# A transformer block on one core: the normed h of the MLP turned by VectorE's 32x32 blocks, with the sum stored in another order and a strided moving side

## The chip, the core and the metric

The kernel runs on one core of a Trainium2 chip. The core has five engines that work at the same time and are tied together by semaphores: TensorE (matmuls and transposes, results into PSUM), VectorE, ScalarE, GpSimd, and SyncE, which here only issues transfers between the chip's memory (DRAM) and the core's own memory (SBUF). In the profile they are PE (with PEld, its loading of weights), DVE, ACT, POOL and SP. The metric is the device time of one execution in microseconds (us); lower is better.

## The reference

An attention block and an MLP, each behind a layernorm, on 2048 tokens of width 1024, all in float32:

```python
h  = x + attention(layernorm(x), wqkv, w_phi, wo)     # 32 heads of 32, feature map by two softmaxes
h2 = h + relu(layernorm(h) @ w1) @ w2                 # w1: 1024 x 3584, w2: 3584 x 1024
```

The change lies between the sum h and the product with w1: h is summed, its mean and variance per token are taken, it is normed, and turned so that the width lies on the 128 partitions (TensorE sums over partitions).

## The kernel before, in words

Each float32 product is made of three products of split operands in the fp32r format: a high part, and the low part that is left (`mm3`, lines 180 to 183: high by high, high by low, low by high). The split costs a copy on ScalarE and a subtraction on VectorE or GpSimd. A 128x512 result lies in one PSUM bank. The banks are named `mm` (4), `tp` (2) and `ac` (2).

The stages, in order of time: projections to k, v and q for all tokens; attention, overlapped with the output projection (`wo_item`, 128 tokens by 512 columns each, eight `mm3`); the MLP's up projection (`up_item`), in two halves b = 0, 1 of 1024 tokens; then its down projection.

Up and down projection use a scheme with seven instead of eight products of quarter matrices (Strassen's, Winograd's form). One half has 1024 tokens and a width of 1024, so it is a matrix of four quarters of 512x512. Seven operands are formed from them: the quarters themselves and sums and differences of them. For the turned h they are called m = 1, 5, 6, 2, 7, 3, 4 (`UP`).

The path of h, tile by tile (a tile has 128 tokens, number t):

- `wo_load` loads x in halves of 512 columns, `wo_add` adds the product to it on VectorE (line 728), `wo_store` stores the half to the DRAM tile `hd[t]`.
- `ln_pair(b, i, stage)` takes two tiles, of the token quarters r = 0 and 1, at the same place i. Eight pairs in all: four with b = 0 beside the output projection, four with b = 1 during the up projection. Stage 0 loads both tiles (line 214), 1 takes the statistics on VectorE (`bn_stats`, line 220), 2 makes scale and bias on GpSimd (lines 229 to 231), 3 norms on ScalarE (line 243). Stages 4 to 7 turn both tiles on TensorE: four groups of four 128x128 transposes (lines 250 and 758) into a `tp` bank, and a copy back by ScalarE (lines 252 and 759). Stage 7 also makes two of the sums on VectorE (lines 760 and 761), stage 8 two more on GpSimd (lines 766 and 767).
- `ln_store` stores the seven operands of the pair to DRAM tiles `hs[b, m]`, `h_load` brings them back by operand and half g into the low part of `hT[m]`, `h_high` and `h_low` split them.
- `up_item` multiplies: the weights w are the stationary side, `hT[m][:, s, k, :]`, 512 contiguous columns (tokens), is the moving side.
- At the end `d_load` loads h from `hd` once more, and `d_add` adds the down projection to it.

The order of the instructions on each engine is written out by hand. TensorE's list of work is made of items. A step is one `mm3` within an item; `when(step, f, ...)` puts a piece of work behind that step. All the other engines get their instructions in the order of these steps, each engine executes its own in that order, and waits stand in that order too. `wo0` and `up0` are the first steps of output and up projection. `LN2` holds the steps of the stages of a pair, counted from `wo0 + 64 + 40 i` for b = 0 and `up0 + 60 + 68 i` for b = 1; its last number is that of the stores.

SP issues nearly all the transfers, in order as well: the raw weights (six buffers, loaded as they come free), x, h, the seven operands, the results.

Of the kernel before, what the change touches and what calls it, by code (L numbers as in the profile page):

```python
# [15 lines left out]
P = 128  # L16
# [123 lines left out]
def kernel(  # L140
# [56 lines left out]
    hd = [dram.tile([P, D], F32, name=f"hd{t}") for t in range(NT)]  # L197
# [17 lines left out]

    def ln_stats(key):
        src = xin[key]
        st = lnp.tile([P, 2, 6], F32, name="st", bufs=4)
# [21 lines left out]
    def ln_norm(key):  # L240
        sc, src = xst.pop(("s", key[1]) if key[0] == "x" and key[1] >= HT else key), xin.pop(key)
        xnt[key] = src if key[0] == "h" else fp_ln.tile([P, D], F32, name="xn")
        act.activation(xnt[key], src, AF.Identity, bias=sc[:, 1:2], scale=sc[:, 0:1])

    def ln_turn(key, j, dst=None):
# [5 lines left out]
        if dst is None:  # L251
            act.activation(xn[:, j * 512:(j + 1) * 512], pt.rearrange("p k n -> p (k n)"), AF.Copy)
            return
# [446 lines left out]
    def wo_load(t, hf):  # L700
        xh[t, hf] = hp.tile([P, 512], F32, name="xh", bufs=5)
        sp.dma_start(xh[t, hf], x[t * P:(t + 1) * P, hf * 512:(hf + 1) * 512])

# [22 lines left out]

    def wo_add(t, hf):
        v.tensor_add(xh[t, hf], wo_ps.pop((t, hf)), xh[t, hf])

    def wo_store(t, hf):  # L730
        sp.dma_start(hd[t][:, hf * 512:(hf + 1) * 512], xh.pop((t, hf)))

    def ln_pair(b, i, stage):

        keys = [("h", HT * b + 4 * r + i) for r in range(2)]
        if stage == 0:
            for key in keys:  # L740
                ln_load(key, [hd[key[1]]])
        elif stage == 1:
            for key in keys:
                ln_stats(key)
        elif stage == 2:
            for key in keys:
                ln_power(key)
        elif stage == 3:
            for key in keys:
                ln_norm(key)  # L750
        elif stage in (4, 5, 6):
            ln_turn(keys[stage // 6], stage != 4)
        elif stage == 7:
            x1, x2 = (xnt[key] for key in keys)
            s12 = (mp or hp).tile([P, 2, 512], F32, name="s12", bufs=1)
            pt = tp_bank()
            for k in range(4):
                pe.transpose(pt[:, k * P:(k + 1) * P], x2[:, k * P:(k + 1) * P], ident)  # L758
            act.activation(x2[:, 0:512], pt, AF.Copy)
            v.tensor_add(s12[:, 0, :], x2[:, 0:512], x2[:, 512:])  # L760
            v.tensor_sub(x2[:, 0:512], x1[:, 0:512], x2[:, 0:512])
            sums[b, i] = s12
        elif stage == 8:
            x1, s12 = xnt[keys[0]], sums[b, i]
            s4 = (mp or hp).tile([P, 512], F32, name="s4l", bufs=1)
            pool.tensor_tensor(out=s12[:, 1, :], in0=s12[:, 0, :], in1=x1[:, 0:512], op=ALU.subtract)
            pool.tensor_tensor(out=s4, in0=x1[:, 512:], in1=s12[:, 1, :], op=ALU.subtract)
            sums[b, i] = s12, s4

    def ln_store(b, i, j):  # L770

        x1, x2 = (xnt["h", HT * b + 4 * r + i] for r in range(2))
        s12, s4 = sums[b, i]
        m, t = ((1, x1[:, 0:512]), (5, s12[:, 0, :]), (6, s12[:, 1, :]), (2, x1[:, 512:]), (7, x2[:, 0:512]),
                (3, s4), (4, x2[:, 512:]))[j]
        sp.dma_start(hs[b, m][:, i, :], t)
# [3 lines left out]
    def h_load(b, m, g):  # L780

        lo = hT[m][:, 1, :, 2 * g * P:2 * (g + 1) * P].rearrange("p k (i n) -> p k i n", i=2)
        for i in range(2):
            sp.dma_start(f32(lo[:, :, i, :]), hs[b, m][:, 2 * g + i, :].rearrange("p (k n) -> p k n", k=4))

    def h_parts(m, g):

        return (hT[m][:, s, :, 2 * g * P:2 * (g + 1) * P] for s in range(2))
# [531 lines left out]
```

## Time and profile before

| | us |
|---|---|
| median of 3 runs | 1881.68 (1880.31 to 1882.74) |
| the profiled execution | 1881.49 |
| its span, from the first to the last instruction | 1879.7 |
| granted clock of TensorE | 1.00 throughout |
| moved by DMA | 433.21 MB |

The profile is of one execution. It lists the busy time of each engine, the groups of instructions by line with count and mean duration, the waits, and the chain of work that ended last, followed back from the last instruction: at each step it goes to what released it, or to the instruction before it on its engine. An engine that isn't on that chain may be idle or busy without a cost. TensorE's matmuls overlap in its pipe: the duration in a group is longer than the distance from one start to the next, and it is the distance that counts. "q1" is SP's DMA queue, "q10" that of ScalarE.

### The profile page before, as it was taken

Reading aid. Unit: us, or ns where it says so; the run is one execution under the profiler, and the core shown is the slowest. Engines: PE = TensorE matmul, PEld = TensorE weight load, DVE = VectorE, ACT = ScalarE, POOL = GpSimd, SP = SyncE. Lnnn points to the kernel's source line nnn. Section 1 sums busy time; section 2 is a strip of 40 time slices with the busy share of each in tenths; the row PEclk is TensorE's granted clock in tenths of the full one; section 3 lists DMA queues with packets and bytes.
Section 4 is the critical chain, followed back from the end, with each engine's and each line's share of the span. In section 5 each row is a group of like instructions: output and inputs, shape, how many; then the busy total and the mean of one; then the engine's idle time right before and its main releaser. Section 6 shows DMA issues by size and latency. Waiting matters only on the chain.

```text
span 1879.7 us, 31869 instructions
## 1 busy us (share of the span) xinstructions
PE 1872.6 (100%) x11630; PEld 1540.3 (82%) x11630; DVE 1063.6 (57%) x1714; ACT 741.0 (39%) x1264; POOL 976.9 (52%) x956
## 2 busy tenths in 40 slices
PE   9999999999999999999999999999999999999999
PEld 7888888888888888888888888888888888888887
DVE  7788688677789777455444664444433333343333
ACT  5322244222233122355455554444444444444442
POOL 3778733677745988223343234445444444444443
PEclk9999999999999999999999999999999999999999
DMA  6889875454475567886877997877877677777775
GB/s 214 268 280 312 269 262 180 148 155 141 140 232 190 203 216 237 264 254 209 263 233 241 312 297 248 264 246 259 275 239 216 201 230 239 237 213 220 216 215 177
DMA packets 293036, 433.21 MB, mean 230 GB/s; under 512 B 24208, under 2 KB 150160, under 8 KB 292880
## 3 DMA queue, kind: packets, MB, share of 16 engines
q1 hardware_dynamic: 263712, 390.26, 65.3%
q10 hardware_dynamic: 29168, 40.93, 6.5%
q8 instruction: 91, 1.49, 0.3%
q14 instruction: 65, 0.53, 0.1%
HBM read 293.73 MB, written 137.36 MB: 229 GB/s over the span
## 4 chain that ended last, share of the span: by engine, by line
PE 98%; DVE 1%; ACT 0%; POOL 0%; DMA 0%; issue 0%; SPq 0%; DVEq 0%; POOLq 0%
PE mm L181 25%; PE mm L182 25%; PE mm L183 25%; PE ac L181 4%; PE ac L182 4%; PE ac L183 4%; PE tp L182 2%; PE tp L181 2%; PE tp L183 2%; PE tp L250 1%; PE tp L678 1%; PE ac L491 1%; PE ac L678 1%; PE tp L297 0%; DVE st L220 0%; PE tp L758 0%
## 5 line engine op out<-in xcount | busy, mean ns | idle before, releaser
L128 POOL TENSOR_TENSOR w<-raw,w 128x512 fp32r<-128x512 f32 x353 | 474.6, 1347 | 671.5 <-ACT w L124 638.0
L124 ACT ACTIVATE w<-raw 128x512 fp32r<-128x512 f32 x686 | 409.1, 626 | 491.8 <-PE mm L183 238.9
L128 DVE TENSOR_TENSOR w<-raw,w 128x512 fp32r<-128x512 f32 x333 | 275.0, 827 | 512.9 <-ACT w L124 507.3
L181 PE MATMUL mm<-w,xT 128*128 128x512 f32 x752 | 299.4, 398 | 0.0
L183 PE MATMUL mm<-w,xT 128*128 128x512 f32 x752 | 293.1, 390 | 0.0
L182 PE MATMUL mm<-w,xT 128*128 128x512 f32 x752 | 293.0, 390 | 0.0
L181 PE MATMUL mm<-hT,w 128*128 128x512 f32 x672 | 262.6, 391 | 0.0
L183 PE MATMUL mm<-hT,w 128*128 128x512 f32 x672 | 261.6, 389 | 0.0
L182 PE MATMUL mm<-hT,w 128*128 128x512 f32 x672 | 261.5, 389 | 0.0
L378 POOL TENSOR_TENSOR b<-b 128x256 f32<-128x256 f32 x168 | 129.0, 769 | 85.2 <-DMA b<-in_w_dram 75.4
L181 PEld LDWEIGHTS mm<-w,xT 128*128 128x128 f32 x752 | 141.2, 188 | 31.4 <-issue 2.2
L183 PEld LDWEIGHTS mm<-w,xT 128*128 128x128 f32 x752 | 141.2, 188 | 30.0
L182 PEld LDWEIGHTS mm<-w,xT 128*128 128x128 f32 x752 | 141.3, 188 | 28.5 <-issue 1.0
L181 PE MATMUL mm<-w 128*128 128x512 f32 x392 | 152.5, 389 | 0.0
L182 PE MATMUL mm<-w 128*128 128x512 f32 x392 | 152.5, 389 | 0.0
L183 PE MATMUL mm<-w 128*128 128x512 f32 x392 | 152.5, 389 | 0.0
L183 PEld LDWEIGHTS mm<-hT,w 128*128 128x128 f32 x672 | 126.1, 188 | 26.5
L181 PEld LDWEIGHTS mm<-hT,w 128*128 128x128 f32 x672 | 126.2, 188 | 25.8
L182 PEld LDWEIGHTS mm<-hT,w 128*128 128x128 f32 x672 | 126.2, 188 | 25.7
L480 POOL TENSOR_TENSOR zacc<-zacc,kphi 128x512 f32<-128x512 f32 x60 | 83.8, 1397 | 14.3 <-DVE kphi L472 14.3
L181 PEld LDWEIGHTS mm<-w 128*128 128x128 f32 x392 | 73.6, 188 | 15.3
L182 PEld LDWEIGHTS mm<-w 128*128 128x128 f32 x392 | 73.6, 188 | 15.3
(173 smaller groups left out, 3183.1 us busy)
## 6 DMA issues: line engine op xcount, KB each, us to landing
raw<-t SPq DMA_DIRECT2D x224, 256.0 KB, 4.0
raw<-ad SPq DMA_DIRECT2D x196, 256.0 KB, 3.0
raw<-in_w_dram SPq DMA_DIRECT2D x168, 256.0 KB, 3.2
ad<-c SPq DMA_DIRECT2D x112, 256.0 KB, 4.2
b<-in_w_dram SPq DMA_DIRECT2D x42, 512.0 KB, 5.7
t<-b SPq DMA_DIRECT2D x42, 512.0 KB, 3.6
ad<-s SPq DMA_DIRECT2D x84, 256.0 KB, 4.6
ed<-qe ACTq DMA_DIRECT2D x32, 512.0 KB, 3.9
```

What stands on the lines that cost most here:

```text
L124: nc.scalar.activation(w[:, 0, :], raw[1], AF.Copy)
L128: eng.tensor_tensor(out=w[:, 1, :], in0=raw[1], in1=w[:, 0, :].bitcast(F32), op=ALU.subtract)
L181: pe.matmul(ps, a_hi, b_hi, start=first, stop=False, skip_group_check=more)
L182: pe.matmul(ps, a_hi, b_lo, start=False, stop=False, skip_group_check=more)
L183: pe.matmul(ps, a_lo, b_hi, start=False, stop=last, skip_group_check=more)
L250: pe.transpose(pt[:, k, :], xn[:, (4 * j + k) * P:(4 * j + k + 1) * P], ident)
L378: pool.tensor_tensor(out=tsum[j, *out], in0=tsum[j, *a], in1=tsum[j, *b], op=ALU.subtract)
L480: pool.tensor_tensor(out=zacc[s], in0=zacc[s], in1=phi_of[key], op=ALU.add)
L491: pe.matmul(kv_ps[s][g][32 * i:32 * (i + 1), 0:64], vt[:, 32 * h:32 * (h + 1)], phi[:, 64 * h:64 * (h + 1)], start=first, stop=last)
L678: pe.matmul(banks[g][32 * c:32 * (c + 1), r * P:(r + 1) * P], kvL[rows, 4 * q + 2 * sd + h // 4, 32 * (h % 4):32 * (h % 4 + 1)], phT[rows, ...
```

## The change

VectorE's `transpose` turns each 32x32 block of a tile in its place. It takes a column inside a block to a row, and leaves the blocks where they are. For the width to come to lie on the partitions in the right order, h is stored so that the loads put the blocks where they are needed.

- `wo_add` writes the sum in another order of columns into a new tile `xo` (2 buffers; `xh` has 3 instead of 5): a column group (k, a, i) of 4 x 4 x 32 becomes (a, k, i). `hd[t]` has the shape 4 x 128 x 2 x 128: block row a, token, half, column.
- The statistics are taken at the sum (`wo_stats`), `wo_power` makes scale and bias on GpSimd, `wo_keep` stores these two numbers per token to the DRAM tiles `shd`.
- `ln_pair` loads each tile in four pieces of 256 columns, in which a partition holds column block a of one in 32 tokens, and the scales four times, with each token's beside its piece. The norm is four instructions of 256 columns, each with its own scale. Then VectorE turns the whole 128x1024 tile in place, twice per pair. The 16 transposes on TensorE per pair and the copies from PSUM go. The sums on VectorE and GpSimd stay, on columns in two-level order.
- `h_load` loads two tiles' operands with one transfer instead of two, into a place where each partition's run is contiguous.
- The moving side of `up_item` is now 16 runs of 32 columns, 128 columns apart. The result comes out in the usual order of tokens.
- `d_load` loads h in its new order into `raw`, and the first `d_add` puts it back.
- The steps of `LN2` and of x's loads are others.

```diff
+    hd = [dram.tile([4, P, 2, P], F32, name=f"hd{t}") for t in range(NT)]
+    shd = {(b, i): dram.tile([P, 2, 2], F32, name=f"shd{b}_{i}") for b in range(2) for i in range(4)}
...
+    def turn_norm(dst, src, scale, bias):
+        for g in range(4):
+            c = slice(256 * g, 256 * (g + 1))
+            act.activation(dst[:, c], src[:, c], AF.Identity, bias=bias(g), scale=scale(g))
...
-        xh[t, hf] = hp.tile([P, 512], F32, name="xh", bufs=5)
+        xh[t, hf] = hp.tile([P, 512], F32, name="xh", bufs=3)
...
+    def by_group(ap):
+        return ap.rearrange("p (k a i) -> p k a i", k=4, a=4)
+    def by_row(ap):
+        return ap.rearrange("p (a k i) -> p k a i", k=4, a=4)
     def wo_add(t, hf):
-        v.tensor_add(xh[t, hf], wo_ps.pop((t, hf)), xh[t, hf])
+        v.tensor_add(by_row(xo[t, hf]), by_group(wo_ps.pop((t, hf))), by_group(xh.pop((t, hf))))
+    def wo_stats(t, hf):
+        st = hst[t]
+        v.bn_stats(out=st[:, 6 * hf:6 * hf + 6], in_=xo[t, hf])
+        if hf:
+            v.bn_aggr(out=st[:, 12:14], in_=st[:, 0:12].rearrange("p (j c) -> p j c", j=2))
+    def h_rows(t, hf):
+        return hd[t].rearrange("a p r c -> p a r c")[:, :, hf, :]
     def wo_store(t, hf):
-        sp.dma_start(hd[t][:, hf * 512:(hf + 1) * 512], xh.pop((t, hf)))
+        sp.dma_start(h_rows(t, hf), xo.pop((t, hf)).rearrange("p (a c) -> p a c", a=4))
+    def wo_power(t):
...
+    def wo_keep(t):
+        sp.dma_start(shd[t // HT, t % 4][:, t % HT // 4, :], hst.pop(t)[:, 14:16])
...
         if stage == 0:
+            for t in tiles:
+                hx[t] = lnp.tile([P, D], F32, name="xin")
+                src = hd[t].rearrange("a (g j) r c -> g a j (r c)", g=4)
+                for g in range(4):
+                    sp.dma_start(hx[t][:, 256 * g:256 * (g + 1)], src[g])
         elif stage == 1:
+            hsr[b, i] = sr = lnp.tile([P, 16], F32, name="st", bufs=4)
+            src = shd[b, i].rearrange("(g j) r c -> j g (r c)", g=4)
+            for a in range(4):
+                sp.dma_start(sr[32 * a:32 * (a + 1)].rearrange("p (g c) -> p g c", g=4), src)
+        elif stage in (2, 3):
+            r, sr = stage - 2, hsr[b, i]
+            turn_norm(hx[tiles[r]], hx[tiles[r]], lambda g: sr[:, 4 * g + 2 * r:4 * g + 2 * r + 1],
+                      lambda g: sr[:, 4 * g + 2 * r + 1:4 * g + 2 * r + 2])
+        elif stage in (4, 5):
+            ht = hx[tiles[stage - 4]]
+            v.transpose(ht, ht)
...
     def h_load(b, m, g):
-        lo = hT[m][:, 1, :, 2 * g * P:2 * (g + 1) * P].rearrange("p k (i n) -> p k i n", i=2)
-        for i in range(2):
-            sp.dma_start(f32(lo[:, :, i, :]), hs[b, m][:, 2 * g + i, :].rearrange("p (k n) -> p k n", k=4))
+        sp.dma_start(f32(h_parts(m, g)[1]), hs[b, m][:, 2 * g:2 * g + 2, :])
...
+    def by_token(ps):
+        return ps.rearrange("p (t j) -> p t j", j=32)
+    def h_chunk(m, s, k):
+        return hT[m][:, s].rearrange("p i (g k j) -> p k (i g) j", g=4, k=4)[:, k]
...
-            mm3(ps, w[:, 0, cols], w[:, 1, cols], hT[m][:, 0, k, :], hT[m][:, 1, k, :],
+            mm3(by_token(ps), w[:, 0, cols], w[:, 1, cols], h_chunk(m, 0, k), h_chunk(m, 1, k),
...
-        do(max(n - 2, wo_first), -1, wo_load, t, hf)
-        when(8 * n + (11 if n < wo_first + 2 else 9), wo_add, t, hf)
+        when(8 * n - 4 if n > wo_first + 1 else wo0, wo_load, t, hf)
+        late_ = 2 if n < wo_first + 2 else 0
+        when(8 * n + 9 + late_, wo_add, t, hf)
+        when(8 * n + 10 + late_, wo_stats, t, hf)
         when(8 * n + (10 if n > order[-3][1] else 14), wo_store, t, hf)
+        if hf:
+            when(8 * n + 12, wo_power, t)
+            when(8 * n + 16, wo_keep, t)
-    LN2 = ((0, 9, 12, 17, 24, 25, 26, 27, 29, 36), (0, 18, 26, 32, 40, 42, 44, 46, 50, 60))
+    LN2 = ((0, 8, 17, 19, 22, 24, 26, 28, 35), (0, 18, 32, 36, 40, 44, 48, 50, 60))
```

More of the change, by code (lines that the diff above doesn't have):

```diff
@@ new lines, in h_rows @@
+    def h_rows(t, hf):
+        return hd[t].rearrange("a p r c -> p a r c")[:, :, hf, :]
+    def wo_store(t, hf):
+        sp.dma_start(h_rows(t, hf), xo.pop((t, hf)).rearrange("p (a c) -> p a c", a=4))
+    def wo_power(t):
+        st = hst[t]
+        pool.tensor_scalar_add(st[:, 14:15], st[:, 13:14], LN_EPS)
+        pool.tensor_tensor(out=st[:, 14:15], in0=st[:, 14:15], in1=half, op=ALU.pow)
+        pool.tensor_scalar(st[:, 15:16], st[:, 12:13], st[:, 14:15], -1.0, op0=ALU.mult, op1=ALU.mult)
@@ L736, in ln_pair @@
+    def wo_keep(t):
+        sp.dma_start(shd[t // HT, t % 4][:, t % HT // 4, :], hst.pop(t)[:, 14:16])
+    hst, hst_pair, xo = {}, {}, {}
     def ln_pair(b, i, stage):
-        keys = [("h", HT * b + 4 * r + i) for r in range(2)]
+        tiles = [HT * b + 4 * r + i for r in range(2)]
         if stage == 0:
-            for key in keys:
-                ln_load(key, [hd[key[1]]])
-        elif stage == 1:
[L743 to L752, printed above, removed]
-        elif stage == 7:
[L754 to L764, printed above, removed]
@@ new lines, in ln_pair @@
+            for t in tiles:
[3 more added lines that the diff above has]
+                    sp.dma_start(hx[t][:, 256 * g:256 * (g + 1)], src[g])
+        elif stage == 1:
+            hsr[b, i] = sr = lnp.tile([P, 16], F32, name="st", bufs=4)
[9 more added lines that the diff above has]
+            v.transpose(ht, ht)
+        elif stage == 6:
+            x1, x2 = (hx[t] for t in tiles)
+            s12 = (mp or hp).tile([P, 2, 512], F32, name="s12", bufs=1)
+            v.tensor_add(by_half(s12[:, 0, :]), h_half(x2, 0), h_half(x2, 1))
+            v.tensor_sub(h_half(x2, 0), h_half(x1, 0), h_half(x2, 0))
+            sums[b, i] = s12
+        elif stage == 7:
+            x1, s12 = hx[tiles[0]], sums[b, i]
@@ L768, in ln_pair, with h_half, by_half @@
             sums[b, i] = s12, s4
+    hx, hsr = {}, {}
+    def h_half(ap, r):
+        return ap.rearrange("p (g r c) -> p g r c", g=4, r=2)[:, :, r, :]
+    def by_half(ap):
+        return ap.rearrange("p (g c) -> p g c", g=4)
     def ln_store(b, i, j):
-        x1, x2 = (xnt["h", HT * b + 4 * r + i] for r in range(2))
+        x1, x2 = (hx[HT * b + 4 * r + i] for r in range(2))
         s12, s4 = sums[b, i]
-        m, t = ((1, x1[:, 0:512]), (5, s12[:, 0, :]), (6, s12[:, 1, :]), (2, x1[:, 512:]), (7, x2[:, 0:512]),
-                (3, s4), (4, x2[:, 512:]))[j]
@@ L786, in h_parts @@
     def h_parts(m, g):
-        return (hT[m][:, s, :, 2 * g * P:2 * (g + 1) * P] for s in range(2))
+        return [hT[m][:, s, 2 * g:2 * g + 2, :] for s in range(2)]
     def h_high(m, g):
```

49 lines of the change are left out of this document (31 added, 18 removed).

## The prediction

> **What bounds the kernel now.** I read the page first, then the chain that ended last in order of time, then the views of single lines, then busy time by stretch.
>
> ```profile
> span 1879.7 us, 31869 instructions
> PE 1872.6 (100%) x11630; PEld 1540.3 (82%) x11630; DVE 1063.6 (57%) x1714; ACT 741.0 (39%) x1264; POOL 976.9 (52%) x956
> PE 98%; DVE 1%; ACT 0%; POOL 0%; DMA 0%; issue 0%; SPq 0%; DVEq 0%; POOLq 0%
> ```
>
> TensorE is busy all the time, which alone would prove little. The third line proves more: of the chain that ended last, 98% is TensorE's own instructions, so nearly the whole time it waits for nobody. What is added to its list lengthens the kernel, what is taken off shortens it, and the other engines count only where they come too late. The profiled run took 1881.49 us, 1.8 us around its span of 1879.7; the median of the runs is 1881.68, so 0.2 us are to be added at the end.
>
> What a step of TensorE costs stands in the chain, in order of time (start us, us, piece). First a turn of a tile pair beside the output projection, then one in the up projection:
>
> ```profile
> 666.84 0.23 PE mm L183
> 667.07 0.44 PE tp L250 x4
> 667.51 0.23 PE mm L181
> 667.74 0.23 PE mm L182
> 667.97 0.23 PE mm L183
> 668.20 0.44 PE tp L250 x4
> ...
> 669.33 0.44 PE tp L250 x4
> ...
> 870.96 0.44 PE tp L250 x4
> ...
> 872.79 0.44 PE tp L250 x4
> ```
>
> A group of four transposes and three matmuls take 668.20 - 667.07 = 1.13 us. For a plain matmul take a long stretch without transposes:
>
> ```profile
> 819.96 0.23 PE ac L181
> ...
> 823.81 0.23 PE ac L183
> ```
>
> These are 17 matmuls apart: 3.85 / 17 = 0.2265 us each. So the group costs 1.13 - 0.68 = 0.45 us in the first stretch. In the second, a group and six matmuls take 1.83 us, the group 0.47 us. (The 0.44 of the row leaves out what the next matmul loses; the 389 ns that the groups by line give for a matmul is its latency in the pipe.)
>
> **The change, part by part.** *Transposes off TensorE.* The turn of the normed h goes.
>
> ```profile
> L250 PE MATMUL tp<-ident,xin 128*128 128x128 f32 x96 | 14.4, 272 | 0.0
> L758 PE MATMUL tp<-ident,xin 128*128 128x128 f32 x32 | 4.8, 272 | 0.0
> ```
>
> That is 128 transposes, 32 groups of four, 16 for the first half of the tokens and 16 for the second: 16 x 0.45 + 16 x 0.47 = 14.7 us off the chain. The last column of both rows is TensorE's idle time ahead of them, nothing: all of it is work.
>
> *The strided moving side.* In its place every matmul of the up projection reads its 512 moving columns as 16 runs of 32 words, 128 words apart. The output bank is written in order, as before.
>
> ```profile
> L181 PE MATMUL mm<-hT,w 128*128 128x512 f32 x672 | 262.6, 391 | 0.0
> L181 PE MATMUL ac<-hT,w 128*128 128x512 f32 x112 | 43.9, 392 | 0.0
> ```
>
> Three lines of each: 3 x (672 + 112) = 2352 matmuls, so 1 ns each is 2.35 us, and 14.7 / 2352 = 6.2 ns each would eat the whole gain. This is the large unknown. No fp32r matmul of this trace has strided columns, but the folding one of L297 has: its moving side is w[rows, :, c, :], eight runs of 32 words, 128 words apart, in plain f32. The first three rows are its first three rounds over the 16 small tiles (timeline: start us, us); the last, from the chain, is a contiguous f32 product of 512 columns, also two instructions:
>
> ```profile
> 77.59 0.40 PE L297 MATMUL tp<-wt,wphi 32*32 32x256 f32 x2
> 77.83 0.38 PE L297 MATMUL tp<-wt,wphi 32*32 32x256 f32 x2
> 78.04 0.59 PE L297 MATMUL tp<-wt,wphi 32*32 32x256 f32 x2
> 373.59 0.86 PE tp L518 x2
> ```
>
> Contiguous, 512 columns take 0.43 us, so 256 take 0.215. Strided, 256 take 0.24 us in one round and 0.21 in the next. From above that bounds the price at 0.025 us for eight runs, 50 ns for a matmul of 16 runs, 118 us in all; from below it is nothing, as the same columns in more pieces can hardly be read faster. I take nothing: the second round is on the contiguous rate to the row's hundredth, and the first also holds the loading of 16 new tiles. The weak points are that plain f32 moves its columns at about half the rate of the up projection, and that a hundredth over eight runs is 1.25 ns per run, 20 ns per matmul, which the row can't exclude.
>
> *What is added off the chain.* Two turns of 128x1024 on VectorE for each of eight pairs, the norm in four pieces of 256 columns on ScalarE, and four copies from PSUM fewer on ScalarE per pair:
>
> ```profile
> L664 DVE STREAM_TRANSPOSE qe<-qe 128x1024 f32<-128x1024 f32 x28 | 34.2, 1227 | 12.1 <-POOL qe L658 9.5 <-POOL qe L648 1.7 <-DMA xh<-in_x_dram 1.0
> L243 ACT ACTIVATE xin<-xin,sc 128x1024 f32<-128x1024 f32 x16 | 19.3, 1236 | 13.5 <-POOL sc L231 12.7 <-DVE oT L695 0.4
> L252 ACT ACTIVATE xin<-tp 128x512 f32<-128x512 f32 x24 | 14.4, 599 | 24.2 <-PE tp L250 22.8 <-DVE qden L643 1.3
> L453 ACT ACTIVATE vt<-mm 128x256 f32<-128x256 f32 x64 | 24.5, 382 | 125.0 <-PE mm L183 125.0
> L728 DVE TENSOR_TENSOR xh<-mm,xh 128x512 f32<-128x512 f32 x32 | 21.1, 665 | 10.0 <-PE mm L183 10.0
> ```
>
> VectorE gains 16 x 1.23 = 19.6 us; ScalarE gains 16 x (4 x 0.38 - 1.24) = 4.5 us and loses 32 x 0.6 = 19.2. The statistics only move from the reloaded tile to the sum (the same 32 of them), GpSimd's power steps move with them, and the adds with regrouped operands have the same 512 columns. All of that is hidden as long as each engine keeps up with TensorE. Busy us of two stretches of 30 us beside the attention (us, PE, PEld, DVE, ACT, POOL, clock, DMA share, GB/s):
>
> ```profile
> 680.00:710.00 30.00, 30.00 (x380) 24.44 (x379) 20.03 (x36) 7.30 (x14) 25.73 (x33) 1.00 0.71 238
> 710.00:740.00 30.00, 30.00 (x380) 24.43 (x379) 23.05 (x40) 7.20 (x14) 27.02 (x34) 1.00 0.67 223
> ```
>
> VectorE stands at 23 of 30 at most. Its new turns add 2.45 us in each 36.6 us, the distance of two pairs in these SP rows (timeline):
>
> ```profile
> 644.18 1.47 SPq L214 DMA_DIRECT2D xin<-hd  x2
> 680.78 4.88 SPq L214 DMA_DIRECT2D xin<-hd  x2
> ```
>
> So VectorE goes from 77% to some 84%; if regrouping doubled the 0.665 us of the adds of L728, of which six lie in that time, it would be at 95%, still under the whole. GpSimd, at 27 of 30, is the tightest: TensorE's 36.6 us shrink by 4 x 0.45 = 1.8, and 90% become 95%. It still fits, narrowly.
>
> *Queues.* Per pair SP issues eight loads of h in quarters and four of the scales instead of two, and two stores of scales that wait for GpSimd's power. Behind them on SP stand the loads of x for the sum, the stores of h, and the raw weights. An issue is some 0.4 us, and on the other hand the up projection's h comes in 28 loads instead of 56. A late x holds VectorE's add, and behind it the turns of the attention. What margin there is shows a turn and the product that uses it, VectorE's timeline first, then the chain:
>
> ```profile
> 709.83 2.36 DVE L664 STREAM_TRANSPOSE qe<-qe 128x1024 f32<-128x1024 f32 x2
> 713.58 0.27 PE tp L678 x8
> ```
>
> The turn ends at 712.19, 1.4 us before its product, here behind the two sums of a pair; that is the tightest place I found. With one more turn of 1.23 us ahead of it, it still holds. The quarters' loads are the other unknown:
>
> ```profile
> xin<-hd SPq DMA_DIRECT2D x16, 512.0 KB, 5.2
> raw<-wpk SPq DMA_DIRECT2D x56, 128.0 KB, 3.3
> ```
>
> Quarters of 128 KB should land like the second row, in 3.3 us and a few more for their turn in the queue. The norm stands 17 steps after the load (40 steps are 36.6 us, so 15.6 us); in the up projection it stands 32 steps of three matmuls after it, 21.8 us. From below the price is nothing, from above what the second rival works out. I take nothing.
>
> *The end.* The last adds only read one operand in regrouped order. The sum is 1881.49 - 14.7 = 1866.8, and with the 0.2 us to the median **1867.0 us**, 0.8% faster.
>
> **The rivals.** *Each run of the moving side costs TensorE a start* (the one that ends slower). A contiguous column takes 226.5 / 512 = 0.44 ns. If each of 16 runs loses one column time, a matmul loses 7.1 ns, all 2352 lose 16.7 us, and the time is 1867.0 + 16.7 = 1883.7, no change. If it loses two, 33.3 us, and the time is 1900. It decides from 6.2 ns per matmul. For it: the up projection moves its columns twice as fast as the L297 rows. Against it: the round of 0.21 us.
>
> *The quarters land late.* The source of each begins with a count of 4 that can't be merged with the next. If such a load runs on 4 of the 16 DMA engines, a pair's 1 MB has a quarter of the rate:
>
> ```profile
> DMA packets 293036, 433.21 MB, mean 230 GB/s; under 512 B 24208, under 2 KB 150160, under 8 KB 292880
> q1 hardware_dynamic: 263712, 390.26, 65.3%
> q10 hardware_dynamic: 29168, 40.93, 6.5%
> ```
>
> 230 GB/s at a share of 0.72 is 20 GB/s for a busy engine, so 256 KB on each of four take 13 us, up to twice that with the other transfers between: 13 to 26 us against the 15.6 that are there. ScalarE's norm, VectorE's turn and behind it the attention's turn would come up to 10 us late. Of these, 6 are covered: 4.6 by the five steps from norm to turn, 1.4 by the margin of the attention. The three pairs beside the attention lose 4 us each, 12 in all: 1879. With no cover they lose 30; with 6 us late at most, nothing.
> The Trainium skill, "DMA: Bandwidth & Descriptors", section "Why a DMA increments its semaphore by 16 and not by 1", has this as its rule: the number of engines is the largest up to 16 that divides the slowest dimension of both sides. By that rule the quarters would run on 4 engines; no load in the trace of before has such a source, so it shows neither.
>
> *GpSimd becomes the bound beside the attention.* If its 5% of room are dependent waits, the 12 groups of the first three pairs give nothing, 12 x 0.45 = 5.4 us: 1872.
>
> **How the numbers follow.** Forecast (1865 to 1871): 0.64. GpSimd or SP's waits keep a part (1871 to 1875): 0.07. Quarters late (1875 to 1882): 0.07. One column time per run (1878 to 1885): 0.09. Two or more, or any other stall of that size (above 1885.4): 0.13. A measurement of this kernel tells 0.2%, 3.8 us, from no change, so faster means below 1877.9. Of the quarters' case about half lies there, and nearly none of the column case. Faster: 0.64 + 0.07 + 0.04 + 0.01 = 0.76; slower 0.13; the rest, 0.11, is no change. The range reaches from 1864.5 (groups worth 0.53 us each) to 1879, into the quarters' case: 0.64 + 0.07 + 0.05 + 0.02 is near 0.8. The 118 us of the first round stay outside of it, with the tail of the column case.
>
> **What would show it.** The span loses 14.7 us, of which about 7 between the first sum of the attention block and the first matmul on hT, and about 7.5 in the up projection. In the chain no transposes remain after 600 us and TensorE keeps 98%. The start distance of the hT matmuls, 0.2265 us, tells of the moving side at once: 0.2265 is the forecast, 0.234 the rival's one column time, 0.241 two. The quarters' time to landing tells of the second: 3 to 6 us or over 12, and then ScalarE's norm waits for DMA. Idle time of TensorE before L678 would be GpSimd's or VectorE's lateness. The prediction is wrong if the hT matmuls lose over 2 ns each, or if TensorE waits anywhere beside the attention or at the first hT matmul.

## The result and the profile after

The changed kernel takes 1937.3 us, the median of 4 runs (1936.39 to 1938.24), where the kernel before takes 1880.99 beside it: a ratio of 1.0299, 95% interval 1.0283 to 1.0315. It is 3% slower. Forecast were 1867.0 us, and the range ended at 1879.

From the page of the changed kernel: the span, busy time by engine, TensorE's busy tenths in 40 slices of 48 us, DMA's totals, and the engines' shares of the chain that ended last.

```profile
span 1935.5 us, 31701 instructions
PE 1894.1 (98%) x11502; PEld 1533.5 (79%) x11502; DVE 1076.4 (56%) x1730; ACT 734.6 (38%) x1280; POOL 978.3 (51%) x956
PE   9999999999999978989999999999999999999999
DMA packets 317420, 433.29 MB, mean 224 GB/s; under 512 B 30672, under 2 KB 185296, under 8 KB 317264
PE 54%; DMA 2%; DVE 1%; SPq 0%; issue 0%; ACT 0%; POOL 0%; DVEq 0%; ACTq 0%
```

Two things are to be seen. TensorE has gaps now, in the 15th to the 18th slice, that is from 677 to 871 us: the end of the attention and the start of the up projection. And although 128 transposes are gone, its busy time has grown from 1872.6 to 1894.1 us. (The chain could be followed back over only 57% of the span, so it isn't used below.)

The two ends of the up projection show where the time lies. First the kernel before, then the changed one (timeline of TensorE: start us, us, instruction): the first and the last matmul on hT.

```profile
802.11 0.39 PE L181 MATMUL mm<-hT,w 128*128 128x512 f32 x1
...
1342.55 0.39 PE L183 MATMUL mm<-hT,w 128*128 128x512 f32 x1
```

```profile
832.04 0.50 PE L181 MATMUL mm<-hT,w 128*128 128x512 f32 x1 [2.79 <-ACT hT L833]
...
1159.15 0.40 PE L181 MATMUL mm<-hT,w 128*128 128x512 f32 x1
1159.39 0.40 PE L182 MATMUL mm<-hT,w 128*128 128x512 f32 x1
...
1169.81 0.40 PE L181 MATMUL mm<-hT,w 128*128 128x512 f32 x1
...
1398.19 0.40 PE L183 MATMUL mm<-hT,w 128*128 128x512 f32 x1
```

| stretch | before | after | difference |
|---|---|---|---|
| up to the first matmul on hT | 802.1 | 832.0 | +29.9 |
| from there to the last one | 540.4 | 566.2 | +25.7 |
| the rest of the span | 537.2 | 537.3 | +0.2 |

From 1159.15 to 1169.81 lie 45 matmuls: 0.2369 us each, against 0.2265 before. To the nanosecond, over the second half of the up projection, the trace has 236.7 ns against 226.7. All 2352 of them at 10.0 ns more are 23.5 us. With the 7.5 us of the transposes taken off, 10 us of the second row are left for waits; in the first row it is 29.9 + 7.2 = 37 us. So 23.5 us are slower matmuls and 47 are waits and what follows from them, against 14.7 us of gain.

How one of these waits comes about is shown by the second pair of tiles. The changed kernel's timeline, engine by engine (in brackets the idle time ahead, and what ended it):

```profile
689.23 8.22 SPq L779 DMA_DIRECT2D xin<-hd  x8
697.49 1.24 SPq L706 DMA_DIRECT2D xh<-in_x_dram  x1
700.45 2.51 SPq L784 DMA_DIRECT2D st<-shd  x4
704.69 2.07 ACTq L591 DMA_DIRECT2D qe<-ed  x2
707.38 3.55 ACT L221 ACTIVATE xin<-xin,st 128x256 f32<-128x256 f32 x7 [14.02 <-DMA st<-shd]
711.33 0.63 ACT L688 ACTIVATE oT<-tp 128x256 fp32r<-128x256 f32 x2
710.79 2.50 POOL L623 TENSOR_TENSOR ez<-qe,zb 128x512 f32<-128x512 f32 x2 [8.24 <-DMA qe<-ed]
712.09 0.69 DVE L630 TENSOR_REDUCE qtz<-ez 128x16 f32<-128x512 f32 x1 [8.26 <-POOL ez L623]
719.77 0.72 DVE L699 TENSOR_TENSOR oT<-tp,oT 128x256 fp32r<-128x256 f32 x2
721.21 0.79 PE L183 MATMUL mm<-w,oT 128*128 128x512 f32 x1 [7.93 <-DVE oT L699]
```

SP is held for 8.2 us by the eight quarter loads. Behind them it issues a load of x (697.49). By the trace's semaphore events, twelve of the sixteen parts of this load have landed by 701.6, the last four only at 704.6. ScalarE's next issue of an attention load (line 591) waits for just this landing, as both transfers count on the same one of eight semaphores; the issue after it waits until 706.4 for a store of the sum. GpSimd waits 8.2 us for the first of these two loads, VectorE 8.3 us for GpSimd, and it reaches line 699, the low part of an attention result, at 719.8. For that TensorE waits 7.9 us.

The norm stands behind the two issues in ScalarE's order. Its row puts the idle time of 14.0 us down to the scales, but they only came last: the issues ahead of it ended at 706.8, the scales landed at 707.3. Behind the norm stands the copy of that attention result (line 688), which is done at 712.5; so the later of the two ways to line 699 is that of the attention load.

The busy time by stretch (us, PE, PEld, DVE, ACT, POOL, granted clock, DMA share, GB/s) adds that the clock falls as well:

```profile
710.00:715.00 5.00, 0.88 (x3) 0.30 (x2) 1.97 (x3) 2.49 (x7) 3.94 (x6) 1.00 0.89 282
715.00:725.00 10.00, 3.79 (x9) 3.02 (x10) 8.48 (x16) 0.00 (x0) 8.35 (x14) 0.50 0.46 132
725.00:730.00 5.00, 5.00 (x99) 3.92 (x104) 4.96 (x6) 0.00 (x0) 4.73 (x6) 0.97 0.01 4
```

From 715.0 to 725.3 TensorE is granted half its clock, and after the pause its matmuls start 0.43 us apart until 725.2. So a wait costs more than its own length. Up to 866 us there are six such stretches, 37.5 us in sum, in which TensorE works for some 27 us. At 0.43 us for a matmul in place of 0.2265 that loses some 13 us, an estimate; its idle time is 34 us longer than before (37.7 us against 3.4). The two make up the 47.

### The profile page after: what moved, and what is told of

The parts are those of the page before. It is cut to its first block, busy times and chain, and to the rows that moved or that the text cites. A ratio compares the mean times of both kernels' runs of the same rounds, so it can differ in the third digit from the quotient of the medians.

```text
span 1935.5 us, 31701 instructions
## 1 busy us (share of the span) xinstructions
PE 1894.1 (98%) x11502; PEld 1533.5 (79%) x11502; DVE 1076.4 (56%) x1730; ACT 734.6 (38%) x1280; POOL 978.3 (51%) x956
## 2 busy tenths in 40 slices
DMA packets 317420, 433.29 MB, mean 224 GB/s; under 512 B 30672, under 2 KB 185296, under 8 KB 317264
## 4 chain that ended last, share of the span: by engine, by line
PE 54%; DMA 2%; DVE 1%; SPq 0%; issue 0%; ACT 0%; POOL 0%; DVEq 0%; ACTq 0%
PE mm L183 12%; PE mm L181 12%; PE mm L182 12%; PE ac L183 4%; PE ac L181 4%; PE ac L182 4%; PE tp L181 2%; PE tp L183 2%; PE tp L182 2%; DMA hd<-xo 1%; DMA hT<-hs 0%; DMA raw<-in_w_dram 0%; DMA hs<-xin 0%; DVE hT L837 0%; DMA st<-shd 0%
## 5 line engine op out<-in xcount | busy, mean ns | idle before, releaser
L181 PE MATMUL mm<-hT,w 128*128 128x512 f32 x672 | 270.0, 402 | 5.3 <-ACT hT L833 2.8
L182 PE MATMUL mm<-hT,w 128*128 128x512 f32 x672 | 269.1, 400 | 2.9 <-DVE hT L837 2.9
L183 PE MATMUL mm<-hT,w 128*128 128x512 f32 x672 | 269.8, 402 | 0.0
L183 PEld LDWEIGHTS mm<-w,xT 128*128 128x128 f32 x752 | 141.2, 188 | 29.9
```

The source lines that it names most:

```text
L181: pe.matmul(ps, a_hi, b_hi, start=first, stop=False, skip_group_check=more)
L182: pe.matmul(ps, a_hi, b_lo, start=False, stop=False, skip_group_check=more)
L183: pe.matmul(ps, a_lo, b_hi, start=False, stop=last, skip_group_check=more)
```

## The experiments

The theory after the first comparison: the slower matmuls come from the 32-word runs, and the waits from the quarter loads, which run on 4 of the 16 DMA engines. The rival: the waits come from what else was added beside the attention (the scales' way through DRAM, two buffers for the sum, GpSimd's steps), and the loads' engines matter little. All medians are in us; each ratio is to the kernel before on the same chip, with its 95% interval.

### The two causes, one at a time and together

*e1: the moving side in one piece.*

```diff
-        return hT[m][:, s].rearrange("p i (g k j) -> p k (i g) j", g=4, k=4)[:, k]
+        return hT[m][:, s, k, :].rearrange("p (t j) -> p t j", j=32)
```

> The changed kernel with the moving side of the up projection read as 512 contiguous columns; nothing else differs, so tokens and width are mixed up in the product. Theory A (16 runs of 32 words cost a matmul 10.2 ns, the start distance goes from 0.2367 to 0.2265 us): 2352 x 10.2 ns = 24 us less, 1913 us, and the start distance of the hT matmuls back at 0.2265 us. Rival (the longer distance comes from somewhere else, such as two-level output or contention): distance stays near 0.237 and the time within 5 us of 1937.

*e2: the quarters read from consecutive rows.*

```diff
-                src = hd[t].rearrange("a (g j) r c -> g a j (r c)", g=4)
+                src = hd[t].rearrange("a p r c -> (a p) (r c)")
...
-                    sp.dma_start(hx[t][:, 256 * g:256 * (g + 1)], src[g])
+                    sp.dma_start(hx[t][:, 256 * g:256 * (g + 1)], src[P * g:P * (g + 1)])
```

> The changed kernel with each quarter of a tile of h loaded from 128 rows that follow each other in DRAM (same bytes, same 1 KB rows, the wrong tokens), so the source no longer begins with a count of 4. Theory B (such a load runs on 4 of 16 DMA engines, and its lateness makes all of the other 47 us: 37 before the first hT matmul, some 9 behind it): 1937 - 47 = 1890 us, first hT matmul at about 795 instead of 832 us, packets under 512 B up by 64 x 12 = 768. Rival C (the waits come from what SP now waits for: GpSimd's scales, x loaded later, two buffers for the sum): 1925 or more.

*e3: both edits.*

> Both edits, contiguous moving side and loads from rows that follow each other. If theories A and B hold and add up, what is left is the removal of the transposes: 1881 - 14.7 = 1866 us, between 1863 and 1871. If C holds in place of B: 1900 or more.

The last two columns of this table and of those that follow (us) are of the profiled execution, one for each kernel.

| | us | ratio | first hT matmul | first to last |
|---|---|---|---|---|
| changed | 1937.3 | 1.0299 [1.0283, 1.0315] | 832.0 | 566.2 |
| e1 | 1922.98 | 1.0226 [1.0206, 1.0246] | 832.0 | 553.3 |
| e2 | 1914.34 | 1.0183 [1.0166, 1.0200] | 812.3 | 560.7 |
| e3 | 1894.74 | 1.0074 [1.0059, 1.0089] | 817.3 | 539.4 |

Both causes are real, but none of the three runs reaches the time that was expected with the theory. In e1 only 13 of the 23.5 us came off the up projection, since the faster matmuls run into operands that are late (TensorE idles 13.1 us there, 5.4 in the changed kernel); with the loads mended as well (e2 to e3) it is 21. The loads alone are worth 23 us. But e3 is not 1867: some 28 us are left that neither cause explains. Small differences in the third column tell little: up to the first matmul on hT, e2 and e3 have the same code and still differ by 5 us.

What the loads do is shown by DMA's share in tenths and its GB/s, in slices of 0.25 us from 688 to 698 us, the changed kernel first, then e3:

```profile
DMA  9999999999995441340131222222222222222222
GB/s 342 346 365 379 387 383 354 363 344 348 342 289 178 129 98 51 29 66 8 66 86 66 61 98 98 98 94 98 98 94 94 94 98 94 98 98 98 98 90 94
```

```profile
DMA  9999999999999956797200177156987999667999
GB/s 367 371 373 367 379 367 350 338 342 316 316 344 273 295 172 225 242 307 254 94 25 20 45 193 262 45 123 233 291 311 230 229 127 119 111 152 264 315 348 342
```

While the quarters are moved, about a quarter of the DMA engines is busy (0.27 from 693 to 698 us), at 94 to 98 GB/s: 1 MB takes 11 us, and little else goes on. The semaphore events show the four: the quarter load issued at 689.23 steps its semaphore once at 690.2 and then four times, from 693.8 to 694.5, where the load of x has sixteen steps. The packets count the same: e2 has 31440 under 512 B, 768 more than the changed kernel's 30672, which is 64 loads with 12 more small packets each, 16 in place of 4. That is what the Trainium skill's rule would make of a count of 4 ("DMA: Bandwidth & Descriptors", "Why a DMA increments its semaphore by 16 and not by 1"); the trace agrees. SP is held as well, though less by far: 3.7 and 6.0 us in e3 for the eight issues of the pairs at 650 and 689 us, 8.5 and 8.2 in the changed kernel.

### What a run costs TensorE

*e4 and e12: the kernel before, with runs of another length r and step s for each operand (`moving` cuts them out).*

```diff
-            mm3(ps, w[:, 0, cols], w[:, 1, cols], hT[m][:, 0, k, :], hT[m][:, 1, k, :],
+            mm3(in_runs(ps, m), w[:, 0, cols], w[:, 1, cols], moving(m, 0, k), moving(m, 1, k),
```

> The kernel before, with the moving side of each of the seven products read in runs of another length, four run lengths apart: 512 (contiguous) for m = 1, 128 for 5, 64 for 6, 32 for 2, 16 for 7, 8 for 3, 4 for 4; columns are mixed up. If each run costs a start of 0.64 ns, the start distances are 0.2265, 0.229, 0.232, 0.237, 0.247, 0.267 and 0.308 us, and the time is 1881 + 54 = 1935 us. If any two-level pattern costs the same, all but the first are 0.237 and the time is 1902 us.

> The kernel before with the moving side of the up projection in runs of r words, s apart, by operand, so that the products are of other columns: 1 (32, 64), 5 (32, 96), 6 (64, 128), 2 (16, 32), 7 (64, 192), 3 (16, 48), 4 (8, 16). If the length of a run sets the price: 1 and 5 near 236.5 ns, 6 and 7 at 226.5, 2 and 3 near 243. If the step between runs does (128 words and less cost): 6 costs too and 7 does not. If the region read does (2048 words earlier in all operands): 1, 2 and 4, with a span of 1024 words, are cheaper than the same runs were.

Each was run once: e4 took 1897.7 us, e12 1894.47. Two products with the same operand follow each other; the table has the distance from one start to the next in the second of them, in ns from the trace (12 matmuls, the same to 0.1 ns in every such pair looked at). In the first of the two it differs by up to 4 ns, for it begins with its predecessor's pace.

| run, words | step, words | ns | | run, words | step, words | ns |
|---|---|---|---|---|---|---|
| one piece | | 226.7 | | 32 | 64 | 238.3 |
| 128 | 512 | 226.7 | | 16 | 64 | 242.8 |
| 64 | 256 | 226.7 | | 16 | 48 | 235.6 |
| 64 | 192 | 226.7 | | 16 | 32 | 240.3 |
| 64 | 128 | 226.7 | | 8 | 32 | 233.8 |
| 32 | 128 | 236.7 | | 8 | 16 | 232.2 |
| 32 | 96 | 231.7 | | 4 | 16 | 236.1 |

Runs of 64 words or more cost nothing. Below that there is a price of 5 to 16 ns, but not one for each run: 64 runs of 8 words are cheaper than 32 of 16, and a step of 96 words is cheaper than 64 or 128. So neither e4's two rules nor any of the three of e12 holds, and what sets the price below 64 words stays open. For the kernel this is enough: 128-word runs are free.

### A changed kernel without the two causes

The sum keeps its order and the turn stays on VectorE in all that follow, in e13 for half of the tiles. *e5* loads by block row and turns out of place, into the usual order of tokens; the first tile goes into the tile that held the sums, the second into the first one's, the sums into the second one's:

```diff
-                src = hd[t].rearrange("a (g j) r c -> g a j (r c)", g=4)
-                for g in range(4):
-                    sp.dma_start(hx[t][:, 256 * g:256 * (g + 1)], src[g])
+                src = hd[t].rearrange("a (g j) r c -> a j g (r c)", g=4)
+                for a in range(4):
+                    sp.dma_start(hx[t][32 * a:32 * (a + 1)].rearrange("p (g c) -> p g c", g=4), src[a])
...
-            v.transpose(ht, ht)
+            src = ht.rearrange("p (g x j) -> p g x j", g=4, x=8)
+            dst = to.rearrange("p (x g j) -> p g x j", g=4, x=8)
+            for g in range(4):
+                v.transpose(dst[:, g], src[:, g])
...
-        return hT[m][:, s].rearrange("p i (g k j) -> p k (i g) j", g=4, k=4)[:, k]
+        return hT[m][:, s].rearrange("p i (k n) -> p k i n", k=4)[:, k]
```

> The changed kernel with each tile's four loads cut by block row a (32 partitions, four runs of 1 KB) instead of by token quarter g, and VectorE's turn written out of place, so that tokens come back into their usual order and the moving side is 4 runs of 128 words. If the two causes are the loads' four engines and the runs of 32 words: packets under 512 B 31440, the turned-h matmuls 0.2265 us apart, the quarters' issues on SP 4 to 6 us per pair instead of 8.5, and a time like that of the run with both causes taken away, 1895 (1889 to 1901). If the loads cut to 32 partitions are no better than those on four engines: 1910 or more. If the out-of-place turn costs VectorE more than 1.23 us per tile, its row shows it.

*e6* adds `xh` 2 and `xo` 3 buffers in place of 3 and 2.

> As e5_byrow, with three buffers for the regrouped sum and two for x in place of two and three. If the sum's two buffers are what remains late (VectorE waits 23.5 us for stores in e3_both, with the attention's turns behind it): VectorE's wait for a store of h goes and the time falls by 8 us or more below e5_byrow. If the scales' round trip is what remains: the same as e5_byrow within 4 us, as ScalarE still waits some 30 us for the scales.

*e7* is e6 with each tile in one load:

```diff
+                sp.dma_start(hx[t], hd[t].rearrange("a (q g) r c -> (a q) (g r c)", g=4))
...
+            dst = to.rearrange("p (x j g) -> p g x j", g=4, x=8)
```

> As e6_xo3, with token 4q+g in place of 32g+q: each tile comes by one load of 128 contiguous rows of 4 KB, the scales' rows become contiguous (64 B), and VectorE's turn writes words 16 bytes apart. If the number of loads and of packets matters: some 3 to 8 us faster than e6_xo3 and packets under 512 B some 6000 fewer. If the turn with words 16 bytes apart takes longer (above 1.5 us per tile), VectorE pays 0.3 us or more per tile beside the attention and it is no faster.

*e8* is e6 without the scales' way:

```diff
-            for a in range(4):
-                sp.dma_start(sr[32 * a:32 * (a + 1)].rearrange("p (g c) -> p g c", g=4), src)
...
+            turn_norm(hx[tiles[r]], hx[tiles[r]], lambda g: half, lambda g: half)
...
-            when(8 * n + 16, wo_keep, t)
```

> As e6_xo3, without the scales' way through memory: nothing is kept and loaded, and the norm uses constants, so the output is not normed by each token's statistics; statistics and power steps are still executed. If the scales' round trip (ScalarE waits for them with the attention's loads queued behind, SP waits for GpSimd's power) is most of what remains: 1868 to 1873, and TensorE shows nearly no idle time between 640 and 830 us. If it is not: within 5 us of e6_xo3.

| | us | ratio | first hT matmul | first to last |
|---|---|---|---|---|
| e5 | 1886.16 | 1.0024 [1.0014, 1.0035] | 806.5 | 541.0 |
| e6 | 1886.26 | 1.0024 [1.0013, 1.0034] | 806.6 | 541.3 |
| e7 | 1886.98 | 1.0032 [1.0021, 1.0044] | 805.4 | 540.3 |
| e8 | 1875.25 | 0.9968 [0.9957, 0.9978] | 806.2 | 532.9 |

e5 is some 9 us better than e3; it differs in the order of the stores and sums too, and which of these helped wasn't separated. e6 gained nothing, although VectorE's wait for the stores of the sum (19.0 us in e5) went. It also gave up a buffer of x, and SP's wait for the sum only moved (26.1 us at the stores and 15.5 at the loads of x in e5, 45.8 at the loads of x in e6), so what the third buffer alone is worth isn't known. e7 was to gain 3 to 8 us by its single loads and gained none; its turn became longer. That this ate the gain is argued, not shown. The rows by line show e5 first, then e7 (busy us, mean ns):

```profile
L797 DVE STREAM_TRANSPOSE s<-xin 128x256 f32<-128x256 f32 x32 | 11.7, 414 | 0.6 <-ACT xin L221 0.5
```

```profile
L794 DVE STREAM_TRANSPOSE s<-xin 128x256 f32<-128x256 f32 x32 | 16.1, 617 | 2.7 <-ACT xin L221 2.7
```

Writing words 16 bytes apart takes VectorE half as long again. e8 settles two points, though it misses the 1868 to 1873 us that were expected. The scales' way, its issues and its waits together, is worth 11.0 us by the medians on the base of e6 (8.4 between the two profiled executions, nearly all of it in the up projection). There the scales do hold the norm: in e6's second pair ScalarE's last issue ahead of it ends at 689.4, and it waits for the scales until 699.8. And the up projection, once its operands come in time, takes 532.9 us, 7.5 less than before, just what 16 groups of 0.47 us were to bring:

```profile
806.18 0.39 PE L181 MATMUL mm<-hT,w 128*128 128x512 f32 x1
...
1339.08 0.39 PE L183 MATMUL mm<-hT,w 128*128 128x512 f32 x1
```

What e8 still loses, it loses beside the attention: 806.2 in place of 802.1 - 7.2 = 794.9.

### What is left beside the attention

*e9* is e6 with mean and variance kept as they are, scale and bias made after the load, for two tiles at once, the scales' loads ahead, and one turn instruction per tile:

```diff
+    def h_power(b, i):
+        sr = hsr[b, i].rearrange("p (t c) -> p t c", c=2)
+        bias, scale = sr[:, :, 0], sr[:, :, 1]
+        pool.tensor_scalar_add(scale, scale, LN_EPS)
+        pool.tensor_tensor(out=scale, in0=scale, in1=half[:, 0:1].to_broadcast([P, 8]), op=ALU.pow)
+        pool.tensor_tensor(out=bias, in0=bias, in1=scale, op=ALU.mult)
+        pool.tensor_scalar_mul(bias, bias, -1.0)
...
-            when(8 * n + 12, wo_power, t)
-            when(8 * n + 16, wo_keep, t)
+            when(8 * n + 13, wo_keep, t)
```

> As e6_xo3, but mean and variance are kept as VectorE makes them, SP's store waits for no GpSimd step, the scales are loaded beside the tiles, and scale and bias are made after that load, for two tiles in one go (8 instead of 16 power steps on GpSimd, four of them beside the attention instead of sixteen); the turn is one instruction per tile. If the scales' path was worth the 11 us that its absence gave: 1872 to 1877, like e8_noscale, with SP's waits for GpSimd's power gone and the up projection's stretch at 533 us instead of 541. If only the memory round trip itself cost: 1880 or more, with ScalarE still waiting for the scales' load.

*e10* moves the steps of the pairs beside the attention (first the even, then the odd ones); *e11* also moves the last two sums of these pairs from GpSimd to VectorE (`eng = pool if b else v`).

```diff
+    LN2 = ((0, 1, 16, 18, 19, 24, 27, 28, 33), (0, 1, 16, 18, 22, 27, 32, 33, 36), (0, 2, 32, 36, 40, 44, 48, 50, 60))
+    POWER = 10, 10, 22
```

> As e9_latepower, with the norm, turns and sums of the pairs beside the attention moved to steps where VectorE has no turn or sum of the attention waiting behind. If VectorE's order is what is left (the product after the attention's turn waits 2 to 5 us per stretch): 3 to 6 us faster than e9_latepower. If GpSimd's load is: the same within 2 us.

> As e10_steps, with GpSimd's two sums of each pair beside the attention done by VectorE (2.6 us less on GpSimd, 1.4 us more on VectorE in each 36.6 us). If GpSimd's load is what is left: 3 to 6 us faster than e10_steps, near 1867. If VectorE is the tighter one: slower than e10_steps.

| | us | ratio | first hT matmul | first to last |
|---|---|---|---|---|
| e9 | 1885.53 | 1.0021 [1.0011, 1.0030] | 805.8 | 539.0 |
| e10 | 1887.32 | 1.0035 [1.0023, 1.0048] | 811.9 | 535.3 |
| e11 | 1885.08 | 1.0017 [1.0007, 1.0027] | 810.6 | 537.4 |

None of the three helped, and e9's up projection came to 539 us, not to the 533 of e8. The wait for the scales had only moved to GpSimd, by e9's waits from 590 to 800 us (us in total, times, longest):

```profile
ACT xin L221 <- POOL st L766: 33.4, 4, 12.6
POOL st L763 <- DMA st<-shd: 12.2, 4, 10.4
```

and SP still stood at its issues (e9's timeline):

```profile
646.03 8.60 SPq L781 DMA_DIRECT2D xin<-hd  x8
655.59 4.84 SPq L786 DMA_DIRECT2D st<-shd  x4
```

*e14* is e9 with one load per tile, as in e7, but the turn writes runs of 32 words, and the order of tokens is put right where the product is read from PSUM:

```diff
-        act.activation(part(i, name), bank[i, m], func)
+        act.activation(by_row4(part(i, name)), by_col4(bank[i, m]), func)
...
+    def by_col4(ap):
+        return ap.rearrange("p (i g q) -> p i q g", i=4, g=4)
```

*e15* adds e11's sums and one load for the scales, `sp.dma_start(sr, src[None].to_broadcast([4, 32, 16]))`. *e13* tests the other way out: the kernel before, with the change for tiles 8 to 15 alone.

> As e9_latepower, with token 4q+g in place of 32g+q, so that each tile is one load of 4 KB rows; the turn writes runs of 32 words and the order of tokens is put right where the product is read from PSUM. SP issues two loads of h per pair instead of eight. If SP was what held the rest: 1870 to 1877, first matmul on the turned h at 797 to 801 us. If not: within 3 us of e9_latepower's 1885.5.

> As e14_fewloads, with the scales by one load instead of four, and GpSimd's two sums per pair beside the attention done by VectorE. If GpSimd's load is the rest: 4 us or more faster than e14_fewloads, down to 1867. If the stretch has no room whichever engine does the work: within 3 us of e14_fewloads.

> The kernel before, with the change made for the second half of the tokens alone (tiles 8 to 15, whose pairs lie in the up projection): their sums regrouped, mean and variance kept, loads cut by block row, turns by VectorE into the usual order of tokens, moving side contiguous; the first half is turned by TensorE as before. If the transposes are worth what the prediction gave them (16 groups of 0.47 us) and the loss lies beside the attention: 1874 (1872 to 1876.5), first matmul on the turned h at 802 us as before, up projection 533 us instead of 540.4. If statistics and stores of the second half's sums disturb the attention too: first such matmul later than 804 us and the time 1877 to 1881.

| | us | ratio | first hT matmul | first to last |
|---|---|---|---|---|
| e13 | 1878.68 | 0.9983 [0.9974, 0.9992] | 803.9 | 536.1 |
| e14 | 1880.59 | 0.9998 [0.9989, 1.0007] | 805.0 | 533.9 |
| e15 | 1873.15 | 0.9963 [0.9949, 0.9976] | 800.3 | 532.9 |

e14 is 4.9 us below e9, short of what was expected if SP were all. The next step is worth another 7.4 us; it took GpSimd's sums and three of the scales' issues away together, and which did more isn't known. On e10's base the sums alone had given 2.2. The hybrid misses the 1874 us at the median (two of its eleven executions took 1874.6 and 1874.7): 3 us of the up projection's gain are lost at its start, where TensorE waits 2.9 us for an operand's low part. That its first matmul on hT comes 1.8 us later than before doesn't show that the attention is disturbed, for in this execution the clock is halved at the very start of the kernel, where nothing was changed (columns as above):

```profile
8.00:11.00 3.00, 3.00 (x16) 3.00 (x15) 0.03 (x1) 1.19 (x2) 1.32 (x2) 0.50 1.04 389
```

Half a clock from 7.9 to 11.4 us costs some 1.6 us by the estimate above. e4 has the same stretch, e12 has not, and with the code of before up to there their first matmuls on hT come at 803.8 and 800.5.

What e15 still lacked is shown by VectorE's timeline:

```profile
700.43 1.19 DVE L795 STREAM_TRANSPOSE s<-xin 128x1024 f32<-128x1024 f32 x1
...
702.99 1.19 DVE L795 STREAM_TRANSPOSE xin<-xin 128x1024 f32<-128x1024 f32 x1
...
705.65 1.53 DVE L799 TENSOR_TENSOR xin<-xin 128x512 f32<-128x512 f32 x1
707.22 1.66 DVE L800 TENSOR_TENSOR xin<-s,xin 128x512 f32<-128x512 f32 x1
708.80 0.68 DVE L806 TENSOR_TENSOR xin<-xin,s 128x512 f32<-128x512 f32 x1
709.52 0.69 DVE L807 TENSOR_TENSOR s4l<-s,xin 128x512 f32<-128x512 f32 x1
710.13 2.36 DVE L668 STREAM_TRANSPOSE qe<-qe 128x1024 f32<-128x1024 f32 x2
```

Both turns and all four sums of the pair stand ahead of the attention's turns (line 668), which start at 710.1. *e16* spreads them, as in e10 but with the power at step 8; *e17* does so with steps 17, 19, 22, 24, 27, 28, 34 for the even and 17, 19, 22, 27, 32, 33, 36 for the odd pairs, power at 10, and loads x at `8 * n - 1`.

> As e15_fewsums, with power and norm of the pairs beside the attention one or two steps earlier, and turns and sums put between the attention's turns (steps 3, 8, 11 and 14 of each 16) in place of one after the other. If VectorE's order of work is what is left: 1867 to 1870, first matmul on the turned h before 798 us. If the earlier norm only waits longer for its load: within 2 us of e15_fewsums's 1873, or above.

> As e15_fewsums, with the sums of every other pair five steps later, behind the attention's turns, and x's loads three steps later, so that SP waits less for their buffers. If SP's standing at x's loads (69 us in e15_fewsums, with the operands' stores behind it) is what is left: 1867 to 1870 and better than e16_spread. If x then comes too late for the sum: VectorE's wait for x's load grows from 7 us and the time is 1874 or more.

e16: 1870.29 (1869.36 to 1873.85), ratio 0.9948 [0.9931, 0.9964]. e17: 1870.83, 0.9945 [0.9931, 0.9960]. The spreading is worth 2 to 3 us at the medians, but its interval overlaps e15's; the later x is worth nothing that can be told from it. e16's first matmul on hT, at 798.5, just misses the 798 that were expected; e17's comes at 797.6. In e16 the attention's turn starts right behind the pair's, at 705.3, as its timeline shows:

```profile
704.16 1.20 DVE L795 STREAM_TRANSPOSE xin<-xin 128x1024 f32<-128x1024 f32 x1
705.28 1.20 DVE L668 STREAM_TRANSPOSE qe<-qe 128x1024 f32<-128x1024 f32 x1
```

and its page, its first and last matmul on hT, and TensorE's waits from 600 to 1400 us are:

```profile
span 1868.7 us, 31597 instructions
```

```profile
798.48 0.39 PE L181 MATMUL mm<-hT,w 128*128 128x512 f32 x1
...
1331.37 0.39 PE L183 MATMUL mm<-hT,w 128*128 128x512 f32 x1
```

```profile
PE tp L682 <- issue: 2.1, 2, 1.5
PE tp L682 <- DVE qe L668: 0.6, 1, 0.6
```

So a version of the change exists that is 0.5% faster than the kernel before, and 67 us faster than the change as it was made. Of the 14.7 us e16 keeps 11.0 by its span: 7.5 in the up projection and 3.6 of the 7.2 beside the attention. For e17 it is 11.2, 6.8 and 4.5.

## Why the prediction was wrong, by its own steps

**What bounds the kernel** was right: what TensorE waits or does longer is what the span grows by (the table by stretches adds up to +55.8 us). **The transposes' 14.7 us** were right as a term: the up projection's 7.5 came out to the tenth in e8, e15 and e16. Beside the attention the 7.2 are paid only as far as nothing is late; 4.5 (e17) is the most that was reached.

**"I take nothing" for the strided moving side** was the first step that failed. It measured 10.0 ns for each matmul, 23.5 us. The rows it was read from were plain f32 at half the column rate and exact to 20 ns per matmul; the text named both weak points and yet let one round of 0.21 us decide, while the other (0.24) gave up to 50 ns. The break-even was 6.2 ns, so a row that can't tell 20 ns was no ground for a choice. The rival of one column time per run came near in size (7.1 ns), but not in mechanism: the price doesn't go with the number of runs.

**"I take nothing" for the queues** was the second, and the larger one: 37 us up to the first matmul on hT, 10 us after it. The quarters' rival had the cause right, four engines, and too low a price: 12 us, 30 with no cover, and the loads cost 23 (e2). The rate was even a little better than it took (11 us for 1 MB against its 13 to 26). What it had wrong is the path: it followed the quarters only through norm and turn, with 6 us of cover on that way. In the second pair they made a load of x and a store of the sum late, and ScalarE's issues of the attention's loads, ahead of the norm, waited for these, with no cover at all. Of the rest of the 47 us the runs price one part: the scales' round trip, which was counted by its issues on SP and never as a wait, cost 11.0 us on e6's base (e6 to e8), mostly by making the up projection's operands late. What is still left wasn't taken apart. That the clock is halved around the longer pauses stood nowhere in the sum.

**GpSimd as the bound** was a rival at 5.4 us. It may have a part: with its two sums and three issues of SP gone, 7.4 us came back (e14 to e15), but which of the two did it isn't known. The prediction missed that the power steps of all sixteen tiles, not eight, now fall beside the attention.

**VectorE's and ScalarE's added work** is hidden, as forecast: the adds with regrouped operands take 667 ns (665 before), the turns 1.22 us. The norm's quarters take 589 ns, not 382; no run shows that this cost anything. On VectorE the order of work may have mattered (e15 to e16, 2.9 us at the medians). **The end** was right: 537.3 us after the last matmul on hT, as before.

## What to carry to other kernels

Where one engine is busy all the time and the others are fed in order, work taken off it pays only if nothing added can stand in front of what that engine needs: list for each added wait what stands behind it on that queue, issues of transfers too, and for each slow transfer which others wait for its engines or its semaphore. Price such a step at the length of the wait it can cause, not at its busy time. And where the whole gain hangs on an access pattern that no row shows at the same rate, the honest forecast has that pattern's price as a range around the break-even, not as nothing.

## What the runs showed of the hardware

- An fp32r matmul of 512 moving columns takes 226.7 ns in one piece and with runs of 64 or 128 words, and 231.7 to 242.8 ns with runs of 4 to 32 words, in no simple order (e4, e12). The Trainium skill ("SBUF — State Buffer", "Specifications (TRN2)") names 16-byte lines, of which two hits each give the full rate; runs of 32 words fill eight such lines each and still cost 10 ns, so that rule doesn't tell this price.
- A load whose slowest count is 4 kept a quarter of the DMA engines busy (94 to 98 GB/s), and held the issuing SP about 1 us for each 128 KB; without that count (e3) it was 0.5 to 0.75 us. A load of x issued behind the quarters had twelve of its sixteen parts down by 701.6 us and the last four at 704.6.
- The transfers of SP and ScalarE share eight semaphores here, and an issue waits until the transfer before it on the same one has landed: in the changed kernel until 704.6 and 706.4 us, and in the trace of the kernel before none of 1441 issues comes earlier.
- A turn by VectorE of 256 columns takes 414 ns into runs of 32 words and 617 ns into words 16 bytes apart; one instruction of 1024 columns takes 1.22 us, in place or into runs.
- Some 5 us after TensorE went quiet at 710 us (two matmuls at 712.5) its granted clock fell to 0.50 and stayed there from 715.0 to 725.3; the matmuls after the pause, from 721.2 on, were 0.43 us apart for 4 us. Other such stretches lasted 3.4 or 6.8 us.
